# A new token order for q and for the stores, late last tokens, and a new condition in the planner of a linear-attention and SoLU kernel

## The chip, the cores and the metric

The kernel runs on one core of a Trainium2 chip. The metric is device time in microseconds (us). Before the change it was 197.02 us (median of three runs, 196.54 to 197.72). Engines are called as the profile calls them: PE is TensorE, PEld its weight loads, DVE VectorE, ACT ScalarE, POOL GpSimd (it issues the loads), SP SyncE (it issues crossbar transposes and most stores).

## The reference, cut to what matters

```python
# q, k, v: [8 batches, 8 heads, 576 tokens, 64]; w_in [512, 1024]; w_out [1024, 512]
kv  = einsum('bhsd,bhse->bhde', k, v)            # no softmax: one 64x64 matrix per head
o   = einsum('bhsd,bhde->bhse', q, kv)
o   = o / sqrt(mean(o*o, -1) + 1e-6) * g_norm
x   = o.transpose(0, 2, 1, 3).reshape(4608, 512) # rows are tokens
h   = x @ w_in
u   = h * softmax(h)
out = layernorm(u) * g_ln @ w_out                # fp32, 4608 x 512
```

## The kernel before

The 4,608 tokens are worked off in nine chunks of 512. Chunk c below 8 holds 512 tokens of batch c; chunk 8 collects the 64 tokens that each batch has left ("last tokens"). Each chunk gives four output tiles of 128 tokens x 512 fp32, 256 KB each. From chunk 4 on, q is turned by a crossbar transpose that SyncE issues. SyncE issues the stores too, all in one queue, in order.

A small planner decides the order: every piece of work has an engine, a length, a rank and the pieces that it needs, and `Plan.order` deals them out by modelled time, then rank.

```python
def load_q(b, hs):                      # runs of 4 tokens, 1 KB each
    nc.gpsimd.dma_start(
        T["q", b].rearrange("p h j d -> p h (j d)")[:, hs],
        q[b, :, 0:512, :].rearrange("h (p j) d -> p h (j d)", j=4)[:, hs])
...
behind = [] if b < 2 else [("h_mm", 0, 0)] if b == 2 else [("h_mm", b - 3, 2 if b == 3 else 0)]
...
def o_mm(c, hf, tag):                   # q times kv; four 64x64 quarters of PE in turn
    ...
    for b in [c] if c < B else range(B):
        cols = slice(0, 128) if c < B else slice(b, 128, B)     # chunk 8: 32 columns, strided
        ...
            nc.tensor.matmul(ts[z][..., pp, :, cols], kvd[rows, b, ...], T["qT", c][rows, ..., cols], ...)
...
def store(c, m):
    j = 2 * (m % 2) + m // 2
    if c < B:
        dst = out[c * S:c * S + 512, :].rearrange("(p j) d -> j p d", j=4)     # dst[j]: 128 x 512
    else:
        dst = out.rearrange("(b s) d -> b s d", b=B)[:, 512:S, :].rearrange("b (p j) d -> j p b d", j=4)
    (nc.scalar if c == NC - 1 and m % 2 else nc.sync).dma_start(dst[j], T["ob", c, m][:, :])
```

The softmax here doesn't subtract the row's maximum and nothing guards it: scores larger than these inputs give would overflow.

Of the kernel before, what the change touches and what calls it, by code (L numbers as in the profile page):

```python
# [89 lines left out]
def kernel(  # L90
# [57 lines left out]
    q_last = big.tile([128, H, 4, D], BF16, name="q_last")  # L148
# [64 lines left out]
    def load_kv(name, src, b, hs):  # L213

        if hs.start == 0:
            T[name, b] = tile_of((name, b), [128, NP, 9, D], BF16)
        nc.gpsimd.dma_start(  # L217
            T[name, b].rearrange("p n i d -> p n (i d)")[:, hs.start // 2:hs.stop // 2],
            src[b, hs].rearrange("(n r) (p i) d -> (r p) n (i d)", r=2, i=9),
        )  # L220

    def load_q(b, hs):
        if hs.start == 0:
            T["q", b] = tile_of(("q", b), [128, H, 4, D], BF16)
        nc.gpsimd.dma_start(  # L225
            T["q", b].rearrange("p h j d -> p h (j d)")[:, hs],
            q[b, :, 0:512, :].rearrange("h (p j) d -> p h (j d)", j=4)[:, hs],
        )

    def load_q_last(b):  # L230
        nc.gpsimd.dma_start(
            q_last[b:128:B].rearrange("p h j d -> p h (j d)"),
            q[b, :, 512:S, :].rearrange("h (p j) d -> p h (j d)", j=4),
        )
# [17 lines left out]
    for b in range(B):  # L252
        at = b - 9.0 if b > 1 else (-2.0, -1.5)[b]
        behind = [] if b < 2 else [("h_mm", 0, 0)] if b == 2 else [("h_mm", b - 3, 2 if b == 3 else 0)]
        for g, hs in enumerate(heads(b)):
            part = 0.1 * g
            n = len(heads(b))
            for i, (name, src) in enumerate((("k", k), ("v", v))):
                plan.add((name, b, g), "pool", 0.75 if n == 1 else 0.6, at + part + 0.01 * i,
                         lambda name=name, src=src, b=b, hs=hs: load_kv(name, src, b, hs),  # L260
                         behind, uses=[(name, b)] if g else [],
                         first=[] if g else [(name, b)], load=2.9 / n if b < 3 else 3.5)
            plan.add(("q", b, g), "pool", 0.9 if n == 1 else 0.7, at + part + (0.02 if b < 2 else 0.1),
                     lambda b=b, hs=hs: load_q(b, hs), behind,
                     uses=[("q", b)] if g else [], first=[] if g else [("q", b)], load=2.7 / n if b < 3 else 3.3)
        plan.add(("q_last", b), "pool", 0.6, 2.0 + 0.5 * b, lambda b=b: load_q_last(b),
                 [("h_mm", 2 + b // 2, 4 * (b % 2))], load=0.5)
# [45 lines left out]
    def qT_mm(c, hf, tag):  # L313

        t = T["qTp", c, hf] = bank((tag,), [128, 4, 2, 128], BF16)
        for h in range(4):
            for y in range(2):
                src = T["q", c][:, 4 * hf + h, 2 * y:2 * y + 2, :].rearrange("p z d -> p (z d)")
                nc.tensor.transpose(t[:, h, y, :], src, ident[:, :])

    def qT_copy(c, hf):
        if hf == 0:
            T["qT", c] = tile_of(("qT", c), [128, H, 2, 128], BF16)
        dst, src = T["qT", c][:, 4 * hf:4 * hf + 4], T["qTp", c, hf][:, :, :, :]
# [5 lines left out]
    def q_turn(c):  # L330

        t = T["qT", c] = tile_of(("qT", c), [128, H, 2, 128], BF16)
        nc.sync.dma_start_transpose(
            t.rearrange("q h y p -> q (h y) p"), T["q", c].rearrange("p h j d -> p (h j d)")
        )

    def o_mm(c, hf, tag):

        ts = [bank((tag,), [128, 2, 2, 128], FP32) for z in range(2)]
        for z in range(2):  # L340
            T["o", c, hf, z] = ts[z]
        for pp in range(2):
            for b in [c] if c < B else range(B):
                cols = slice(0, 128) if c < B else slice(b, 128, B)
# [345 lines left out]
```

## Time and profile before

| | before |
|---|---|
| time (median); span of the profiled run, which itself took 194.98 us | 197.02; 193.1 us |
| PE busy, granted clock | 179.8 us (93%), 0.998 |
| PE idle between its first and last matmul (gaps over 0.15 us) | 7.2 us |
| last matmul to the end | 4.25 us |

### The profile page before, as it was taken

The numbers are of one execution on the slowest core, as the hardware profiler recorded it, in microseconds if no ns is written. First come the engines' busy times: TensorE is split into PE (matmuls) and PEld (weight loads), VectorE is DVE, ScalarE is ACT, GpSimd is POOL, SyncE is SP. The second block draws the span as 40 slices with busy tenths as digits, with TensorE's granted clock in tenths as the row PEclk, the third lists the DMA queues.
The fourth block names the chain that finished last, engine by engine and source line by source line (L and its number), as shares of the span: only waits on it lengthen the run. The fifth ranks groups of instructions, "written<-read, shape, count | busy, mean of one in ns | idle before, by whom it ended". The sixth has DMA issues, their size and how long they took to land.

```text
span 193.1 us, 5442 instructions
## 1 busy us (share of the span) xinstructions
PE 179.8 (93%) x2282; PEld 88.3 (46%) x2282; DVE 122.6 (63%) x241; ACT 141.0 (73%) x245; POOL 127.9 (66%) x136
## 2 busy tenths in 40 slices
PE   7897997898899998999899999999999999999991
PEld 2352454553354643544354435445445554544460
DVE  1456588468684887496477658567575747666450
ACT  2038888869895997799689987989789496655520
POOL 7981799500999987977499776568285838846200
PEclk9999999999999999999999999999999999999999
DMA  1999999999996999899999996363111111211206
GB/s 22 204 204 266 357 203 205 206 224 248 233 201 86 147 190 258 113 185 168 292 214 200 212 111 182 108 116 114 54 54 58 58 54 58 109 58 54 110 7 213
DMA packets 36040, 29.71 MB, mean 154 GB/s; under 512 B 11816, under 2 KB 30512, under 8 KB 36016
## 3 DMA queue, kind: packets, MB, share of 16 engines
q0 software_dynamic: 20112, 17.30, 56.4%
q1 hardware_dynamic: 15616, 11.67, 22.4%
q10 hardware_dynamic: 288, 0.39, 0.6%
q8 instruction: 18, 0.29, 0.6%
q14 instruction: 6, 0.05, 0.1%
HBM read 32.51 MB, written 9.44 MB: 217 GB/s over the span
## 4 chain that ended last, share of the span: by engine, by line
PE 64%; DMA 20%; ACT 7%; POOL 4%; DVE 2%; issue 2%; SPq 0%; POOLq 0%; DVEq 0%; ACTq 0%
PE out_ps L582 26%; PE h_ps L468 24%; DMA w_out_f<-in_moe_w_out_dram 9%; DMA v_sb<-in_v_dram 7%; PE misc_ps L534 4%; DMA out_dram<-ob_sb 4%; PE s_ps L369 3%; PE o_ps L348 2%; ACT e_sb L476 2%; PE misc_ps L291 1%; DVE u_sb L483 1%; ACT osq_sb L363 1%; ACT rst_sb L377 1%; ACT lss_sb L373 1%; PE h_ps L592 1%
## 5 line engine op out<-in xcount | busy, mean ns | idle before, releaser
L468 PE MATMUL h_ps<-x_sb,w_in_sb 128*128 128x512 bf16 x276 | 70.3, 379 | 3.0 <-DVE u_sb L483 1.7
L582 PE MATMUL out_ps<-w_out_sb,u_sb 128*128 128x512 bf16 x272 | 69.0, 379 | 0.5 <-issue 0.5
L494 POOL TENSOR_TENSOR usq_sb<-u_sb 128x512 bf16<-128x512 bf16 x50 | 52.0, 1042 | 25.5 <-DVE u_sb L483 25.4
L483 DVE TENSOR_TENSOR u_sb<-h_ps,e_sb 128x512 bf16<-128x512 f32 x69 | 47.3, 688 | 30.4 <-ACT e_sb L476 29.5
L500 POOL TENSOR_TENSOR es_sb<-e_sb 128x512 bf16<-128x512 f32 x36 | 45.9, 1274 | 21.6 <-ACT e_sb L476 21.2
L476 ACT ACTIVATE e_sb<-h_ps,zero_t 128x512 f32<-128x512 f32 x69 | 47.1, 684 | 12.6 <-PE h_ps L468 11.8
L468 PEld LDWEIGHTS <-w_in_sb 128*128 128x128 bf16 x288 | 27.3, 98 | 37.5 <-issue 6.9
L582 PEld LDWEIGHTS <-u_sb 128*128 128x128 bf16 x280 | 26.1, 98 | 31.0 <-issue 2.0
L363 ACT ACTIVATE osq_sb<-o_ps,zero_t 128x512 bf16<-128x512 f32 x31 | 20.1, 683 | 15.3 <-PE o_ps L348 15.3
L614 DVE TENSOR_SCALAR ob_sb<-out_ps,rstd 128x512 f32<-128x512 f32 x33 | 24.6, 745 | 10.0 <-PE out_ps L582 4.3
L390 DVE SCALAR_TENSOR_TENSOR x_sb<-o_ps,g_rep,rst_sb 128x512 bf16<-128x512 f32 x32 | 23.9, 749 | 8.6 <-ACT rst_sb L377 8.4
L377 ACT ACTIVATE rst_sb<-lss_sb,zero_t 128x512 f32<-128x512 f32 x32 | 23.2, 726 | 0.7
L373 ACT ACTIVATE lss_sb<-s_ps,eps_t 128x512 f32<-128x512 f32 x32 | 22.0, 688 | 2.2 <-PE s_ps L369 2.2
L492 ACT ACTIVATE usq_sb<-u_sb,zero_t 128x512 bf16<-128x512 bf16 x22 | 15.8, 719 | 5.4 <-DVE u_sb L483 5.4
L369 PE MATMUL s_ps<-osq_sb,head_mean 128*128 128x512 bf16 x34 | 12.9, 380 | 0.3 <-ACT osq_sb L363 0.3
L534 PEld LDWEIGHTS <-stat_sel 128*32 128x32 bf16 x720 | 10.1, 97 | 3.8 <-issue 3.8
L217 POOL DMA_DIRECT2D k_sb<-in_k_dram x10 | 7.8, 784 | 4.3 <-DMA w_in_sb<-in_moe_w_in_dram 2.9
L198 PE MATMUL s_ps<-zeros 128*128 128x512 bf16 x28 | 9.2, 453 | 1.4 <-DVE zero_t L163 1.2
L225 POOL DMA_DIRECT2D q_sb<-in_q_dram x10 | 8.6, 856 | 2.5 <-DMA w_in_sb<-in_moe_w_in_dram 1.5
L348 PE MATMUL o_ps<-qT_sb,kvd 64*64 64x32 bf16 (+1 forms) x240 | 8.2, 256 | 1.1 <-DMA qT_sb<-q_sb 0.7
L291 PEld LDWEIGHTS <-k_sb 64*64 64x64 bf16 x576 | 6.7, 107 | 4.9 <-issue 4.9
L291 PE MATMUL misc_ps<-v_sb,k_sb 64*64 64x64 bf16 x360 | 7.6, 194 | 0.8 <-DMA v_sb<-in_v_dram 0.7
(85 smaller groups left out, 131.6 us busy)
## 6 DMA issues: line engine op xcount, KB each, us to landing
out_dram<-ob_sb SPq DMA_DIRECT2D x34, 256.0 KB, 2.9
k_sb<-in_k_dram POOLq DMA_DIRECT2D x6, 576.0 KB, 13.3
v_sb<-in_v_dram POOLq DMA_DIRECT2D x6, 576.0 KB, 14.3
q_sb<-in_q_dram POOLq DMA_DIRECT2D x6, 512.0 KB, 15.9
w_out_f<-in_moe_w_out_dram POOLq DMA_DIRECT2D x1, 2048.0 KB, 16.5
k_sb<-in_k_dram POOLq DMA_DIRECT2D x4, 288.0 KB, 11.5
v_sb<-in_v_dram POOLq DMA_DIRECT2D x4, 288.0 KB, 12.2
q_sb<-in_q_dram POOLq DMA_DIRECT2D x4, 256.0 KB, 12.2
```

Source lines behind the costliest of these rows:

```text
L363: nc.scalar.activation(out=t[:, :], in_=T[("o", *i)].rearrange("p a b c -> p (a b c)"), func=AF.Square, bias=zero_t[:, :])
L369: nc.tensor.matmul(t[:, :], head_mean[:, :], T["osq", i][:, :], start=True, stop=True)
L373: nc.scalar.activation(out=t[:, :], in_=T["s", i][:, :], func=AF.Ln, bias=eps_t[:, :])
L377: nc.scalar.activation(out=t.rearrange("p a b c -> p (a b c)"), in_=T["lss", i][:, :], func=AF.Exp, scale=-0.5, bias=zero_t[:, :])
L390: nc.vector.scalar_tensor_tensor(out=T["x", c][:, 2 * hf:2 * hf + 2, z], in0=T["o", c, hf, z][:, :, :, :], scalar=g_rep[:, :], in1=T["rst" ...
L468: nc.tensor.matmul(t[:, :], w_in_sb[:, dt, f * 128:(f + 1) * 128], T["x", c][:, dt].rearrange("p a b c -> p (a b c)"), start=(dt == 0), st ...
L476: nc.scalar.activation(out=T["e", c, f // 2][:, f % 2, :], in_=T["h", c, f][:, :], func=AF.Exp, bias=zero_t[:, :])
L483: nc.vector.tensor_tensor(out=T["u", c][:, f, :], in0=T["h", c, f][:, :], in1=T["e", c, f // 2][:, f % 2, :], op=MUL)
L494: nc.gpsimd.tensor_tensor(out=dst, in0=src, in1=src, op=MUL)
L500: nc.gpsimd.tensor_tensor(out=T["es", c][:, n, :], in0=e[:, 0, :], in1=e[:, 1, :], op=ADD)
L582: nc.tensor.matmul(T["acc", c, m][:, :], T["u", c][:, f, m * 128:(m + 1) * 128], w_out_sb[:, f, :], start=(f == 0), stop=(f == NF - 1),)
L614: nc.vector.tensor_scalar_mul(out=t[:, :], in0=T["acc", c, m][:, :], scalar1=T["rstd", c][:, m:m + 1])
```

## The change

The intent: longer runs of q (2 KB in place of 1 KB), the products of the last tokens without stride, the last tokens loaded later, and the loads of chunks 5 to 7 held back until the transpose ahead of them has been issued, because a transpose beside loads was seen to take 12 to 15 us (11.8 and 14.5 us from issue to landing, in the trace of before). Tokens are therefore dealt out in runs of nine (eight for the chunk, the ninth for chunk 8), and the stores follow that order. The core of the diff, cut:

```diff
-        nc.gpsimd.dma_start(
-            T["q", b].rearrange("p h j d -> p h (j d)")[:, hs],
-            q[b, :, 0:512, :].rearrange("h (p j) d -> p h (j d)", j=4)[:, hs],
+            src[b, hs].rearrange("(n r) (p j) d -> (r p) n (j d)", r=2, j=9)[:, :, 0:js * D],
     def load_q_last(b):
-            q_last[b:128:B].rearrange("p h j d -> p h (j d)"),
-            q[b, :, 512:S, :].rearrange("h (p j) d -> p h (j d)", j=4),
+        nc.gpsimd.dma_start(q_last[:, :, b, :], q[b].rearrange("(n r) (p j) d -> (r p) n j d", r=2, j=9)[:, :, 8, :])
...
-        behind = [] if b < 2 else [("h_mm", 0, 0)] if b == 2 else [("h_mm", b - 3, 2 if b == 3 else 0)]
+        behind = ... + ([("turned", b - 1)] if b - 1 in XBAR else [])
...
-        plan.add(("q_last", b), "pool", 0.6, 2.0 + 0.5 * b, ..., [("h_mm", 2 + b // 2, 4 * (b % 2))], load=0.5)
+        plan.add(("q_last", b), "pool", 0.7, 4.0 + 0.25 * b, ..., [("h_mm", 4 + b // 4, 2 * (b % 4))], load=0.7)
...
+            plan.add(("turned", c), "wait", 2.0, r - 0.05, lambda: None, [("q", c, 0)] if c < B else [])
...                                                   # o_mm: chunk 8 by run, 64 contiguous columns
-                cols = slice(0, 128) if c < B else slice(b, 128, B)
+            for y in [slice(0, 4)] if c < B else range(4):
...
+    def rows_of(c, z, y):
+        if c < B:
+            return out[c * S:c * S + S, :].rearrange("(p j) d -> j p d", j=9)[2 * y + z:2 * y + z + 3:2]
+        return out.rearrange("(b p j) d -> j b p d", p=64, j=9)[8, 2 * y + z:2 * y + z + 3:2]
     def store(c, m):
-        ... dma_start(dst[j], T["ob", c, m][:, :])          # 128 x 512
+        ... dma_start(rows_of(c, m // 2, 2 * (m % 2)), T["ob", c, m][:, :])   # 2 x 64 x 512
```

The two halves of the last tile of chunk 8 (`store_cols`) go through `rows_of` as well.

More of the change, by code (lines that the diff above doesn't have):

```diff
@@ L147 @@
     kvd = big.tile([128, B, 2, NP, D], BF16, name="kvd")
-    q_last = big.tile([128, H, 4, D], BF16, name="q_last")
+    q_last = big.tile([128, NP, B, D], BF16, name="q_last")
     g_rep = big.tile([128, 1], FP32, name="g_rep")
@@ L210, with load @@
     plan.add("ident", "pool", 1.0, -1.95, make_ident)
-    def load_kv(name, src, b, hs):
+    def load(name, src, b, hs):
+        js = 8 if name == "q" else 9
         if hs.start == 0:
-            T[name, b] = tile_of((name, b), [128, NP, 9, D], BF16)
+            T[name, b] = tile_of((name, b), [128, NP, js, D], BF16)
         nc.gpsimd.dma_start(
-            T[name, b].rearrange("p n i d -> p n (i d)")[:, hs.start // 2:hs.stop // 2],
-            src[b, hs].rearrange("(n r) (p i) d -> (r p) n (i d)", r=2, i=9),
-        )
-    def load_q(b, hs):
-        if hs.start == 0:
-            T["q", b] = tile_of(("q", b), [128, H, 4, D], BF16)
-        nc.gpsimd.dma_start(
-            T["q", b].rearrange("p h j d -> p h (j d)")[:, hs],
-            q[b, :, 0:512, :].rearrange("h (p j) d -> p h (j d)", j=4)[:, hs],
+            T[name, b].rearrange("p n j d -> p n (j d)")[:, hs.start // 2:hs.stop // 2],
+            src[b, hs].rearrange("(n r) (p j) d -> (r p) n (j d)", r=2, j=9)[:, :, 0:js * D],
         )
     def load_q_last(b):
-        nc.gpsimd.dma_start(
-            q_last[b:128:B].rearrange("p h j d -> p h (j d)"),
-            q[b, :, 512:S, :].rearrange("h (p j) d -> p h (j d)", j=4),
-        )
+        nc.gpsimd.dma_start(q_last[:, :, b, :], q[b].rearrange("(n r) (p j) d -> (r p) n j d", r=2, j=9)[:, :, 8, :])
     def load_w_in(half):
@@ L253 @@
         at = b - 9.0 if b > 1 else (-2.0, -1.5)[b]
-        behind = [] if b < 2 else [("h_mm", 0, 0)] if b == 2 else [("h_mm", b - 3, 2 if b == 3 else 0)]
+        behind = [] if b < 2 else [("h_mm", 0, 0)] if b == 2 else [("h_mm", b - 3, 2 if b == 3 else 0)] + ([("turned", b - 1)] if b - 1 in XBAR else [])
         for g, hs in enumerate(heads(b)):
@@ L257 @@
             n = len(heads(b))
-            for i, (name, src) in enumerate((("k", k), ("v", v))):
-                plan.add((name, b, g), "pool", 0.75 if n == 1 else 0.6, at + part + 0.01 * i,
-                         lambda name=name, src=src, b=b, hs=hs: load_kv(name, src, b, hs),
+            for i, (name, src) in enumerate((("k", k), ("v", v), ("q", q))):
+                plan.add((name, b, g), "pool", (0.8 if name == "q" else 0.75) if n == 1 else 0.6, at + part + (0.01 * i if i < 2 else 0.02 if b < 2 else 0.1),
+                         lambda name=name, src=src, b=b, hs=hs: load(name, src, b, hs),
                          behind, uses=[(name, b)] if g else [],
-                         first=[] if g else [(name, b)], load=2.9 / n if b < 3 else 3.5)
-            plan.add(("q", b, g), "pool", 0.9 if n == 1 else 0.7, at + part + (0.02 if b < 2 else 0.1),
-                     lambda b=b, hs=hs: load_q(b, hs), behind,
-                     uses=[("q", b)] if g else [], first=[] if g else [("q", b)], load=2.7 / n if b < 3 else 3.3)
-        plan.add(("q_last", b), "pool", 0.6, 2.0 + 0.5 * b, lambda b=b: load_q_last(b),
-                 [("h_mm", 2 + b // 2, 4 * (b % 2))], load=0.5)
+                         first=[] if g else [(name, b)], load=(2.55 if name == "q" else 2.9) / n if b < 3 else 3.2 if name == "q" else 3.5)
+        plan.add(("q_last", b), "pool", 0.7, 4.0 + 0.25 * b, lambda b=b: load_q_last(b),
+                 [("h_mm", 4 + b // 4, 2 * (b % 4))], load=0.7)
     for half in range(2):
@@ L313, in qT_mm @@
     def qT_mm(c, hf, tag):
-        t = T["qTp", c, hf] = bank((tag,), [128, 4, 2, 128], BF16)
-        for h in range(4):
-            for y in range(2):
-                src = T["q", c][:, 4 * hf + h, 2 * y:2 * y + 2, :].rearrange("p z d -> p (z d)")
-                nc.tensor.transpose(t[:, h, y, :], src, ident[:, :])
+        t = T["qTp", c, hf] = bank((tag,), [128, 2, 4, 128], BF16)
+        for n in range(2):
+            for y in range(4):
+                src = T["q", c][:, 2 * hf + n, 2 * y:2 * y + 2, :].rearrange("p z d -> p (z d)")
+                nc.tensor.transpose(t[:, n, y, :], src, ident[:, :])
     def qT_copy(c, hf):
         if hf == 0:
-            T["qT", c] = tile_of(("qT", c), [128, H, 2, 128], BF16)
-        dst, src = T["qT", c][:, 4 * hf:4 * hf + 4], T["qTp", c, hf][:, :, :, :]
+            T["qT", c] = tile_of(("qT", c), [128, NP, 4, 128], BF16)
+        dst, src = T["qT", c][:, 2 * hf:2 * hf + 2], T["qTp", c, hf][:, :, :, :]
         if c == 1:
@@ L330, in q_turn @@
     def q_turn(c):
-        t = T["qT", c] = tile_of(("qT", c), [128, H, 2, 128], BF16)
+        t = T["qT", c] = tile_of(("qT", c), [128, NP, 4, 128], BF16)
         nc.sync.dma_start_transpose(
-            t.rearrange("q h y p -> q (h y) p"), T["q", c].rearrange("p h j d -> p (h j d)")
+            t.rearrange("q n y p -> q (n y) p"), T["q", c].rearrange("p n j d -> p (n j d)")
         )
     def o_mm(c, hf, tag):
-        ts = [bank((tag,), [128, 2, 2, 128], FP32) for z in range(2)]
+        ts = [bank((tag,), [128, 2, 4, 64], FP32) for z in range(2)]
         for z in range(2):
@@ L342, in o_mm @@
         for pp in range(2):
-            for b in [c] if c < B else range(B):
-                cols = slice(0, 128) if c < B else slice(b, 128, B)
+            n = 2 * hf + pp
+            for y in [slice(0, 4)] if c < B else range(4):
                 for hh in range(2):
@@ L348, in o_mm @@
                         nc.tensor.matmul(
-                            ts[z][hh * 64:hh * 64 + 64, pp, :, cols], kvd[rows, b, hh ^ z, 2 * hf + pp, :],
-                            T["qT", c][rows, 4 * hf + 2 * pp + hh, :, cols], start=True, stop=True,
+                            ts[z][hh * 64:hh * 64 + 64, pp, y, :], kvd[rows, c if c < B else 2 * y + z, hh ^ z, n, :],
+                            T["qT", c][rows, n, y, 64 * hh:64 * hh + 64], start=True, stop=True,
                         )
@@ L375, in s_exp @@
     def s_exp(*i):
-        t = T["rst", i] = tile_of(("rst", i), [128, 2, 2, 128], FP32)
+        t = T["rst", i] = tile_of(("rst", i), [128, 2, 4, 64], FP32)
         nc.scalar.activation(
@@ L381, in s_rsqrt @@
     def s_rsqrt(*i):
-        t = T["rst", i] = tile_of(("rst", i), [128, 2, 2, 128], FP32)
+        t = T["rst", i] = tile_of(("rst", i), [128, 2, 4, 64], FP32)
         nc.scalar.activation(
@@ L388, in x_mul @@
         if (hf, z) == (0, 0):
-            T["x", c] = tile_of(("x", c), [128, NP, 2, 2, 128], BF16)
+            T["x", c] = tile_of(("x", c), [128, NP, 2, 4, 64], BF16)
         nc.vector.scalar_tensor_tensor(
@@ L429 @@
             kvs = [("kv", b, x, part) for b in ([c] if c < B else range(B)) for x in ((hf,) if b < 2 else range(2)) for part in range(3)]
-            plan.add(("o_mm", c, hf), "pe", 0.25 if c < B else 1.2, r + w * (0.35 + 0.5 * hf),
+            plan.add(("o_mm", c, hf), "pe", 0.25 if c < B else 0.6, r + w * (0.35 + 0.5 * hf),
                      lambda c=c, hf=hf, tag=tag: o_mm(c, hf, tag), [("qT", c) if c in XBAR else ("qT", c, hf), *kvs],
@@ L605, in store_cols @@
     def store_cols(x):
-        dst = out.rearrange("(b s) (x d) -> b s x d", b=B, x=2)[:, 512:S, x, :].rearrange("b (p j) d -> j p b d", j=4)[3]
-        (nc.sync, nc.scalar)[x].dma_start(dst, T["ob", NC - 1, 3][:, x])
+        cols = slice(x * d_model // 2, (x + 1) * d_model // 2)
+        (nc.sync, nc.scalar)[x].dma_start(
+            rows_of(NC - 1, 1, 2)[:, :, cols], T["ob", NC - 1, 3][:, x]
+        )
     def scale(c, m):
@@ L614, in scale @@
             nc.vector.tensor_scalar_mul(out=t[:, :], in0=T["acc", c, m][:, :], scalar1=T["rstd", c][:, m:m + 1])
+    def rows_of(c, z, y):
+        if c < B:
+            return out[c * S:c * S + S, :].rearrange("(p j) d -> j p d", j=9)[2 * y + z:2 * y + z + 3:2]
+        return out.rearrange("(b p j) d -> j b p d", p=64, j=9)[8, 2 * y + z:2 * y + z + 3:2]
     def store(c, m):
-        j = 2 * (m % 2) + m // 2
-        if c < B:
-            dst = out[c * S:c * S + 512, :].rearrange("(p j) d -> j p d", j=4)
-        else:
-            dst = out.rearrange("(b s) d -> b s d", b=B)[:, 512:S, :].rearrange("b (p j) d -> j p b d", j=4)
-        (nc.scalar if c == NC - 1 and m % 2 else nc.sync).dma_start(dst[j], T["ob", c, m][:, :])
+        (nc.scalar if c == NC - 1 and m % 2 else nc.sync).dma_start(
+            rows_of(c, m // 2, 2 * (m % 2)), T["ob", c, m][:, :]
+        )
     plan.add("w_mean", "pe", 2.0, -0.5, lambda: [w_mean(f) for f in range(NF)], ["w_out", "g_mean", ("o_mm", 0, 1)],
```

## The prediction

> **What bounds the kernel now.** I read the page first: shares by engine, then the chain that ended last, then PE's gaps in the timeline, then each DMA's issue and landing, because the change touches loads, crossbar transposes and stores.
>
> ```profile
> PE 179.8 (93%) x2282; PEld 88.3 (46%) x2282; DVE 122.6 (63%) x241; ACT 141.0 (73%) x245; POOL 127.9 (66%) x136
> ```
>
> PE is the bound: 179.8 of a 193.1 us span, at a granted clock of 0.998. The other 13.3 us are 1.2 before the first matmul, 4.25 after the last one (188.87 to 193.12: last scaling and last stores), and gaps inside. From the timeline the gaps over 0.15 us add to 7.2 us, and 5.3 of those lie before 48 us. What ended the gaps that the change could touch, from the view of waits:
>
> ```profile
> PE misc_ps L291 <- DMA v_sb<-in_v_dram: 0.7, 1, 0.7
> PE o_ps L348 <- DMA qT_sb<-q_sb: 0.7, 1, 0.7
> DVE ob_sb L614 <- DMA out_dram<-ob_sb: 2.0, 1, 2.0
> ```
>
> The second is chunk 5's crossbar transpose (gap at 94.3 us). The third is its after-effect: VectorE waits for a store, and PE loses 0.37 us more at 96.6. SyncE's timeline from 60 to 100 us shows why:
>
> ```profile
> 61.37 1.70 SPq L333 DMA_TRANSPOSE qT_sb<-q_sb  x1
> 68.02 5.04 SPq L623 DMA_DIRECT2D out_dram<-ob_sb  x3
> 80.37 7.29 SPq L333 DMA_TRANSPOSE qT_sb<-q_sb  x1
> 87.76 3.44 SPq L623 DMA_DIRECT2D out_dram<-ob_sb  x4
> ```
>
> The transpose at 61.37 meets chunk 5's loads (issued 61.58 to 63.99) and lands after 11.8 us, chunk 5's q only at 80.32; the next transpose meets chunk 6's loads (78.43 to 80.88) and lands after 14.5 us. The one of the last chunk, with the queue empty, lands after 4.3. So the intent is sound, and worth about 0.67 + 0.37 = 1.04 us.
>
> Now the stores, which the diff changes only in passing. Windows of the trace: one around a single store, one with only stores running, one in the stage of loads.
>
> ```profile
> 138.10:139.00 0.90, 0.90 (x6) 0.42 (x5) 0.14 (x1) 0.90 (x2) 0.00 (x0) 1.00 0.75 291
> 140.00:165.00 25.00, 25.00 (x308) 12.47 (x307) 16.67 (x29) 19.16 (x33) 16.64 (x15) 1.00 0.14 55
> 5.00:35.00 30.00, 26.27 (x355) 13.64 (x353) 18.74 (x32) 19.11 (x32) 23.41 (x28) 1.00 1.28 239
> ```
>
> The last two columns are the mean busy share of the 16 DMA engines and GB/s. One 256 KB store takes 0.75 x 0.9 us = 0.675 us of all sixteen, so 10.8 engine-us. That agrees with the packet records: 128 packets of 2 KB at a median 84 ns, eight to an engine, one behind the other. (1 KB packets: 46 ns.) In the stage of loads the engines are full.
>
> [...] the small load of the norm weights has 8 rows outermost, and its semaphore gets one update at 2.66 us and eight at 6.08 to 6.32, with eight data packets and eight completion packets. Ordinary stores have 128 outermost, those of the last chunk 16 (16 x 8 rows): 16 updates each. [...] the first store (38.67 us), beside loads, needs 6.7 us for eight packets per engine, some 0.7 us a packet[...]; alone a store lands in 2.0 us. [...] 64 matmuls of 32 columns take 1.06 us of PE's chain, 8 of 256 columns (as many columns in all) 0.34.
>
> **The change, part by part.**
>
> *The last chunk's products.* 2 x 64 matmuls of 32 columns, read at a stride, become 2 x 32 of 64 contiguous columns. At the same time per instruction (1.06/64 = 16.6 ns) a group takes 0.53 us; the floor is 0.34. PE saves 2 x 0.53 to 0.72, say 1.2 us, all on the path.
>
> *q in runs of eight.* 512 rows of 2 KB per chunk replace 1,024 of 1 KB. In the loads alone (chunk 4) v takes 2.79 us between landings, q 2.66; at v's rate per byte (1.18 MB against 1.05 MB) q would take 2.5. So 0.15 us per chunk: PE's 0.72 us wait for chunk 2's v shrinks by two such, 0.3 us, of which a dependency behind it may eat part. I count 0.2.
>
> *Last tokens.* 8 DMAs of 128 rows of 1 KB become 8 of 512 rows of 256 B, issued later. From 60 ns (1,024 B) and 107 ns (2,304 B) per packet a straight line gives about 32 ns: 32 packets per engine, 1.0 us each, an estimate. Before, the transpose of these tokens landed at 131 and was used at 144.5, so 10 us of room remain.
>
> *Loads behind the transpose.* In the built order chunk 5's and 6's loads move behind one more square and one more sum on GpSimd (1.03 + 1.26 = 2.3 us); a transpose alone needs 4.3, so most of the collision goes: the 1.04 us above.
>
> So far 197.0 - 1.2 - 0.2 - 1.0 = 194.6 us.
>
> *The stores.* The 128 rows of a tile are now tokens 2y+z and 2y+z+2 of 64 runs, and the built stores have an output pattern of 2 x 64 x 512 where before it was 128 x 512 (or 16 x 8 x 512). [...] k = 2, and always the same two engines. One store is then 64 packets per engine, 64 x 84 ns = 5.4 us, where PE delivers a tile every 4.3 us (17.3 us per chunk of four). All work of these two engines from the first store (38.7 us, first packet 0.9 later):
> - stores: 35 x 64 x 84 ns = 188.2, two half ones 2 x 64 x 46 ns = 5.9: 194.1 us
> - loads still to come: 2.5 (chunk 2's q) + 5 x 8.0 = 42.5 (every load needs all engines, these two as well)
> - last tokens: 8.0; five transposes, 128 packets of 256 B per engine at 18 ns: 5 x 2.3 = 11.5
> Sum 256.1. Loads and stores add rather than overlap: between 41.4 and 53.3 us loads worth 8.2 us took 11.9 with four stores beside them, 0.9 us a store where 0.67 is its own time.
>
> Do these engines rest? Four output buffers and two PSUM banks let PE run six tiles ahead at most, so the ring always holds stores; a transpose stands in the ring behind up to four of them (21.5 us), and PE waits for it in order. Only SyncE's hand-over after each of five transposes lets them idle: 3 us in all, my guess. 38.7 + 0.9 + 256.1 + 3 = 298.7 us of span; time is 3.9 above the span before (197.0 against 193.1), so 302.6, rounded to 303. PE's gains vanish behind that.
>
> **The rivals.** (a) [...] For: the change is plainly meant for a gain; no store in this trace has an outermost 2. Against: the 8-row load is split by eight [...]. Time 194.6. (b) Two engines, but other ones for each store. A store lands after 0.8 + 5.4 + 0.4 = 6.6 us instead of 2.0; four buffers at 4.3 us each tolerate 17, so only the tail grows by some 5: about 200. [...] (c) Two engines, and more starvation than I count: packets at 90 or 100 ns, idle at each transpose. 10 ns more is 35 x 64 x 0.01 = 22 us: 325. (d) Faster packets in long runs: at 76 ns, -18 us: 285.
>
> **Range and chances.** I give k = 2 on fixed engines 0.8. Within it (c) and (d) span 285 to 325; I widen to 275 to 330. The rest goes mostly to (a), which lies within 2% (193.1 to 201.0) more often than under it, and (b).
>
> **What would show it.** Right: stores of 256 KB that land after 6 us or more everywhere (before: 2.0 to 2.4 in the quiet part), with two completion packets each; DMA share about 2/16 = 0.12 throughout the second half, while GB/s stays near 49; PE below 65% busy, its waits on DVE's scaling and on qT_sb; DVE's scaling waiting on out_dram. Matmul groups of the last chunk at about 0.5 us show the first step, chunk 5's q landing well before 80 us (in case (a)) the fourth. Wrong: stores still landing after 2 us; then the time is 194 to 196, and the step that failed is the choice of engines. If two engines are used and the time is under 260, the failed step is that their work adds up without overlap.

Passages on the hardware that no trace of this case shows have been cut from the prediction. Its sum came to 38.7 + 0.9 + 256.1 + 3 = 298.7 us of span, 302.6 as a time. What goes is the reason for k = 2 (k is the number of DMA engines that carry one store). That an outermost 2 means two engines, the same two for every store, was the assumption. Rival (a) is that this form of the stores does no harm.

## More of the kernel before

The prediction shows the lines on PE's share and its waits. Here are the other lines that the change will move, from the page of the kernel before: the busy tenths of PE and of the DMA engines and PE's granted clock, each in 40 slices of the span, then the queue that SyncE's stores and transposes use (packets, MB, share of 16 engines' time), then the chain that ended last.

```profile
PE   7897997898899998999899999999999999999991
PEclk9999999999999999999999999999999999999999
DMA  1999999999996999899999996363111111211206
...
q1 hardware_dynamic: 15616, 11.67, 22.4%
...
PE 64%; DMA 20%; ACT 7%; POOL 4%; DVE 2%; issue 2%; SPq 0%; POOLq 0%; DVEq 0%; ACTq 0%
```

PE is full from end to end, and the DMA engines are full in the first 60% of the span and nearly idle after (1 is 10 to 20%).

## The result, and the profile after

The changed kernel is correct and takes 294.06 us (median of four runs, 293.47 to 295.06); the kernel before took 197.37 us in the same rounds. The ratio is 1.4925 (95% interval 1.4843 to 1.5007). A run counts as slow when it is over 1.5% above the fastest run of its kernel, and as fast otherwise. Ratios here are always the mean time of one kernel's fast runs over the mean of the other's fast runs of the same rounds, so they are not quite the ratio of the medians.

The page of the kernel after, in the same order as the lines of before:

```profile
PE 194.3 (67%) x2218; PEld 92.0 (32%) x2218; DVE 122.4 (42%) x241; ACT 142.2 (49%) x245; POOL 128.7 (44%) x136
...
PE   7889797999224991099708966994599798630000
...
PEclk9999999999955897559986997899599999785555
DMA  6999999919915399579474296178311111111111
...
q1 hardware_dynamic: 15126, 11.67, 34.0%
...
DMA 75%; PE 8%; DVE 4%; ACT 2%; POOL 2%; issue 1%; SPq 0%; DVEq 0%; POOLq 0%
```

The span grew by 98.6 us (193.1 to 291.7), in three parts. PE's gaps add to 61.8 us (before 7.2): +54.6. The last matmul ends at 257.98, so the tail is 33.7 us (before 4.25): +29.5. And PE is busy 14.5 us longer for fewer products, because the granted clock sinks after gaps (the row of clocks; the mean over the span, tail included, is 0.846, and a 128x512 matmul of the first layer takes 408 ns on average in place of 379). The chain has turned from PE (64%) to DMA (75%).

The trace's sixteen clock records are 1.0 or 0.5, none between, and the last window below has 0.50 with no matmul at all. A value between, in a slice or a window, is a mean of the two.

The waits that ended those gaps (who waited for what: us in total, times, longest):

```profile
DVE ob_sb L605 <- DMA out_dram<-ob_sb: 67.4, 18, 8.0
...
PE o_ps L335 <- DMA qT_sb<-q_sb: 33.9, 4, 13.7
PE h_ps L457 <- DVE u_sb L472: 12.3, 6, 5.6
...
PE o_ps L335 <- DMA qT_sb<-q_last: 6.5, 1, 6.5
```

DVE waits 67.4 us for an output buffer, that is for a store to finish, where before it was once 2.0 us; PE waits 33.9 us for the crossbar transposes of the chunks (before 0.7) and 6.5 us for that of the last tokens. SyncE's timeline (start, length, source line, what, count) shows that both are one thing:

```profile
70.20 18.22 SPq L320 DMA_TRANSPOSE qT_sb<-q_sb  x1
88.53 9.61 SPq L615 DMA_DIRECT2D out_dram<-ob_sb  x4
98.25 23.07 SPq L320 DMA_TRANSPOSE qT_sb<-q_sb  x1
121.41 4.87 SPq L615 DMA_DIRECT2D out_dram<-ob_sb  x3
126.39 23.49 SPq L320 DMA_TRANSPOSE qT_sb<-q_sb  x1
```

A transpose stands 13 to 23 us at SyncE (all five; 1.6 to 7.3 before), behind the stores that were issued ahead of it: with the stores cut in two and all else as here (experiment 2) it is 1.6 to 7.1 us. And the windows of 20 us (busy time by engine, then clock, DMA share, GB/s), first a stretch with only stores and PE running, then one in the tail:

```profile
220.00:240.00 20.00, 18.48 (x160) 8.66 (x159) 11.64 (x22) 11.87 (x20) 12.31 (x11) 1.00 0.14 52
...
260.00:280.00 20.00, 0.00 (x0) 0.00 (x0) 0.82 (x2) 1.16 (x2) 0.00 (x0) 0.50 0.13 51
```

In the tail nothing runs but stores, and the sixteen DMA engines are 0.13 busy: two of sixteen, moving 51 GB/s. A tile of 256 KB at 51 GB/s takes 5.1 us.

How many engines carry a store can be read from the packets. Data packets of the stores are as many as before (4,352 of 2 KB). The queue lost 15,616 - 15,126 = 490 packets = 35 stores x 14, all of them packets of 4 bytes (888 before, 398 after): each of SyncE's 35 stores sends two completion packets and not sixteen. (ScalarE's queue lost 28, two stores x 14.) The same count is used in the experiments.

### The profile page after: what moved, and what is told of

It reads as the page before. It is cut to its first block, busy times and chain, and to the rows that moved or that the text cites. A ratio compares the mean times of both kernels' runs of the same rounds, so it can differ in the third digit from the quotient of the medians.

```text
span 291.7 us, 5310 instructions
## 1 busy us (share of the span) xinstructions
PE 194.3 (67%) x2218; PEld 92.0 (32%) x2218; DVE 122.4 (42%) x241; ACT 142.2 (49%) x245; POOL 128.7 (44%) x136
## 3 DMA queue, kind: packets, MB, share of 16 engines
q1 hardware_dynamic: 15126, 11.67, 34.0%
## 4 chain that ended last, share of the span: by engine, by line
DMA 75%; PE 8%; DVE 4%; ACT 2%; POOL 2%; issue 1%; SPq 0%; DVEq 0%; POOLq 0%
DMA out_dram<-ob_sb 60%; DMA qT_sb<-q_sb 7%; DMA qT_sb<-q_last 5%; DMA v_sb<-in_v_dram 2%; PE out_ps L571 2%; PE h_ps L457 2%; DVE ob_sb L605 1%; DVE u_sb L472 1%; POOL k_sb L218 1%; DVE w_out_sb L562 1%; PE misc_ps L198 1%; PE out_ps L556 1%; PE o_ps L457 1%; DVE x_sb L377 1%; PE o_ps L335 1%
## 5 line engine op out<-in xcount | busy, mean ns | idle before, releaser
L457 PE MATMUL h_ps<-x_sb,w_in_sb 128*128 128x512 bf16 x276 | 77.2, 408 | 13.7 <-DVE u_sb L472 12.3
L571 PE MATMUL out_ps<-w_out_sb,u_sb 128*128 128x512 bf16 x272 | 75.1, 401 | 4.1 <-DVE u_sb L472 3.2
L457 PEld LDWEIGHTS <-w_in_sb 128*128 128x128 bf16 x288 | 28.6, 103 | 53.0 <-issue 26.7
L571 PEld LDWEIGHTS <-u_sb 128*128 128x128 bf16 x280 | 27.1, 101 | 38.6 <-issue 7.8
L335 PE MATMUL o_ps<-qT_sb,kvd 64*64 64x256 bf16 (+1 forms) x176 | 7.8, 275 | 41.1 <-DMA qT_sb<-q_sb 33.9
L335 PEld LDWEIGHTS <-kvd 64*64 64x64 bf16 x192 | 4.0, 116 | 49.0 <-issue 41.4
L356 PE MATMUL s_ps<-osq_sb,head_mean 128*128 128x512 bf16 x34 | 13.9, 409 | 0.6 <-ACT osq_sb L350 0.6
L523 PEld LDWEIGHTS <-stat_sel 128*32 128x32 bf16 x720 | 11.1, 103 | 4.4 <-issue 4.4
L218 POOL DMA_DIRECT2D q_sb<-in_q_dram x10 | 7.5, 749 | 3.2 <-DMA w_in_sb<-in_moe_w_in_dram 1.4
## 6 DMA issues: line engine op xcount, KB each, us to landing
w_out_f<-in_moe_w_out_dram POOLq DMA_DIRECT2D x1, 2048.0 KB, 16.5
```

The lines of the kernel that those rows point to most:

```text
L218: nc.gpsimd.dma_start(T[name, b].rearrange("p n j d -> p n (j d)")[:, hs.start // 2:hs.stop // 2], src[b, hs].rearrange("(n r) (p j) d -> ...
L457: nc.tensor.matmul(t[:, :], w_in_sb[:, dt, f * 128:(f + 1) * 128], T["x", c][:, dt].rearrange("p a b c -> p (a b c)"), start=(dt == 0), st ...
L571: nc.tensor.matmul(T["acc", c, m][:, :], T["u", c][:, f, m * 128:(m + 1) * 128], w_out_sb[:, f, :], start=(f == 0), stop=(f == NF - 1),)
```

## The experiments

The first two questions: is it really the outermost size of the store, and what do the other parts do when the stores are mended? Then: does one slow store hurt, or only many; what is the tail worth; is the planner's condition good; and what would be a good version?

### 1. The outermost size alone, on the kernel before

```diff
+        rows = dst[j]
+        if c < B:
+            rows = rows.rearrange("(p a) d -> a p d", a=2)      # also a=4, a=8
-        ... dma_start(dst[j], T["ob", c, m][:, :])
+        ... dma_start(rows, T["ob", c, m][:, :])
```

The 128 rows of a tile are only walked in another order, so the result is wrong; everything else is the kernel before. Chunk 8 keeps its own pattern.

> The kernel before, its layout and order untouched, with the stores of chunks 0 to 7 given an outermost 2 (output pattern 2 x 64 x 512: every second row in each half; the rows land permuted, so the result is wrong on purpose). Theory: two engines carry 32 stores of 5.0 us (the rate seen after), 160 us, beside 43 us of loads, 4 of last tokens and 11.5 of transposes, from 43 us on: some 262 us of span, time 258 to 278. If the form of the stores is not the cause but the layout of q or the order: 196 to 199.

> The same with an outermost 4 (4 x 32 x 512, rows permuted, wrong on purpose). Theory: four engines, 2.5 us a store; PE makes a tile in 4.3 us, so these engines have 80 + 58 = 138 us of work in the 150 us after the first store and are no longer the bound, but some transposes and loads come later: 197 to 206 us. If an outermost dimension under 16 is a penalty of its own (not a share of engines): as slow as with 2, over 255.

> Before, its stores' 128 rows walked as 8x16x512 (rows permuted, so a wrong result on purpose); third point of the dose. If eight engines take a store (16 packets each, 16 x 80 ns = 1.3 us + 1.4 us of latency) it lands after about 2.7 us in the quiet part in place of 2.0-2.3, transposes behind it land later by under a microsecond each: 196-199, ratio 1.005-1.02, where two engines gave 1.415 and four 1.098. Rival: the outermost size acts only through a threshold (a store slower than the interval between tiles), and eight is as good as 128: 0.995-1.005.

| outermost size (chunks 0 to 7) | time, us | ratio to before (95%) | packets lost by SyncE's queue |
|---|---|---|---|
| 128 (before) | 195.62 / 195.74 | 1 | 0 |
| 8 | 202.99 (200.49 to 211.91) | 1.0333 (1.0268 to 1.0398) | 256 = 32 x 8 |
| 4 | 214.12 (213.07 to 216.00) | 1.0983 (1.0913 to 1.1054) | 384 = 32 x 12 |
| 2 | 275.89 (274.88 to 276.50) | 1.4149 (1.4080 to 1.4218) | 448 = 32 x 14 |

(Sizes 4 and 2 ran beside runs of before at 195.62 us, size 8 beside 195.74.) The queue's line in the pages of 8, 4 and 2:

```profile
q1 hardware_dynamic: 15360, 11.67, 30.8%
```

```profile
q1 hardware_dynamic: 15232, 11.67, 32.6%
```

```profile
q1 hardware_dynamic: 15168, 11.67, 32.8%
```

The bytes are the same in all, and each store of 32 sends exactly 8, 4 or 2 completion packets: the outermost size is the number of engines. Size 2 alone, on the old kernel, gives 80 us of the 97. That settles the main cause.

My expectations for 4 and 8 were too low. I had thought of the mean load of the engines; what counts is the stage in which loads run too. Worked out afterwards, as an estimate, for one of the engines used and one chunk of 17.3 us: loads 8.0, one transpose 2.3, last tokens 1.1 (2.3 such loads a chunk, 8 packets an engine at 60 ns each), and four stores at 128/k packets of 80 ns each: 2.6, 5.1, 10.2 or 20.5 us for 16, 8, 4 and 2 engines. The sums are 14.0, 16.5, 21.6 and 31.9 us, so 81%, 95%, 125% and 184% of the chunk. At 125% the four chunks of this stage must lose 4 x 4.3 = 17 us; 18.5 were measured. At 95%, by this estimate, only queueing is left, and the kernel lost 7 us. In both, part of the loss is PE's clock, which falls after a wait (0.957 to 0.964 in the runs of size 4, 0.982 to 0.990 in the fast ones of size 8), so the 17 is closer to the 18.5 than the estimate deserves. The view of waits for size 4 shows where the loss is felt:

```profile
PE o_ps L348 <- DMA qT_sb<-q_sb: 13.9, 3, 4.7
...
DVE ob_sb L614 <- DMA out_dram<-ob_sb: 7.1, 1, 7.1
```

PE waits three times for a transpose, 4.7 us each at most, although over all the chunks together the engines have time enough (138 us of work in 150, in my expectation). (The profile of size 8 fell in its slowest execution, so I read only its counts.)

### 2. The change with each store cut in two

```diff
-        engine.dma_start(dst, T["ob", c, m][:, :])
+        for i in range(2):                                      # 64 x 512 each; store_cols likewise
+            engine.dma_start(dst[i], T["ob", c, m][64 * i:64 * i + 64, :])
```

> The changed kernel with each store cut in two of 64 rows (outermost 64 instead of 2), nothing else. Theory (the 2 x 64 x 512 form puts every store on the same two DMA engines, and these are the bound): stores land after 2 to 3 us again, with 16 completion packets each, PE over 92% busy, time 194.6 us by the steps of the prediction, 193.5 to 197. Rival A (the loads of q in runs of eight, or the last tokens in 256 B rows, choke the DMA engines): still 280 to 295. Rival B (the new order makes the crossbar transposes wait): still over 250, with PE waiting for qT_sb.

197.86 us (six runs, 192.71 to 199.02), correct, above the 193.5 to 197 that I expected; stores land after 2.2 to 2.4 us in the quiet part. Five of the six runs are over 1.5% above the fastest and count as slow, the profiled one (197.58) too, so there is no ratio. But the 97 us are gone, with the change otherwise whole. What is left is not the gain that I had counted on, and the next run says why.

### 3. The same without the planner's condition

```diff
-        behind = ... + ([("turned", b - 1)] if b - 1 in XBAR else [])
+        behind = ...                                            # as before
```

> The cut stores without the planner's new condition (loads of chunks 5 to 7 no longer behind the transpose of the chunk ahead). If the order is worth what the prediction says (0.67 + 0.37 us of PE's waits at one transpose), this is about 1.0 us slower than the cut stores alone, and a transpose beside loads lands after more than 10 us again. If the order is worth nothing: within 0.3 us.

194.03 us (193.39 to 194.43, six fast runs), ratio 0.9939 (0.9904 to 0.9974). So the condition does not save the microsecond. Whether it costs something can't be told from this pair alone: the medians are 3.8 us apart, but five of the six runs with the condition count as slow, and the sixth (192.71) is below all six here. The fast runs of experiment 4 show that it costs; the traces show how. Lines of SyncE's timeline, first with the condition (experiment 2), then without:

```profile
79.75 1.60 SPq L320 DMA_TRANSPOSE qT_sb<-q_sb  x1
...
96.84 7.06 SPq L320 DMA_TRANSPOSE qT_sb<-q_sb  x1
```

```profile
75.67 3.19 SPq L320 DMA_TRANSPOSE qT_sb<-q_sb  x1
...
92.73 2.58 SPq L320 DMA_TRANSPOSE qT_sb<-q_sb  x1
```

With the condition, the transpose of chunk 4 is indeed short (it lands after 3.7 us in place of 15.0). But the loads of chunk 5, held back until 65.0 us, land at 79.7 in place of 75.3, those of chunk 6 at 96.8 in place of 92.7, and then chunk 6's transpose is issued at 96.84, in the middle of chunk 7's loads (96.65 to 98.2), and lands after 15.9 us in place of 4.6. PE waits for it, in the view of waits of experiment 2:

```profile
PE o_ps L335 <- DMA qT_sb<-q_sb: 2.6, 1, 2.6
```

PE loses more than this wait. A window of the same trace (columns as before: busy time by engine, clock, DMA share, GB/s) shows the clock after it:

```profile
114.00:118.00 4.00, 4.00 (x12) 1.50 (x11) 1.44 (x2) 2.32 (x4) 0.74 (x2) 0.59 1.84 233
```

The clock is at half for 3.4 us, from 113.8 us on, which costs some 1.7 us more (half of that stretch, an estimate). In the profile without the condition PE never waits for a transpose, and the clock is full until after the last matmul. One collision was moved from a place with slack to a place without.

### 4. The condition alone, on the kernel before

```diff
+        behind = ... + ([("turned", b - 1)] if b - 1 in XBAR else [])
+            plan.add(("turned", c), "wait", 2.0, r - 0.05, lambda: None, [("q", c, 0)] if c < B else [])
```

> The kernel before with only the planner's new condition (the loads of chunks 5 to 7 put behind the crossbar transpose of the chunk ahead); layout and stores of before. My prediction's step: 1.0 us faster than before, 194.6, ratio 0.995. Theory after e1_split against e3_no_turn (197.9 against 194.0): the condition makes a load wait where it need not, the transpose itself then lands no earlier, and it costs 1 to 4 us, at least in part of the executions: 196.5-199.5, ratio 1.005-1.02, with a gap of TensorE of over 1.5 us before an o_mm that waits for qT.

198.12 us (196.38 to 199.89, six runs, two of them slow), ratio 1.0148 (1.0089 to 1.0207) to a kernel before at 194.80. These are fast runs against fast runs, so here the condition's cost is shown, and the profiled execution (198.01) is a fast one. It is the same picture on the old layout: chunk 6's transpose issued at 99.44 among chunk 7's loads (96.5 to 99.0), landing after 13.3 us, and one new gap of PE of 2.75 us at 110.06, with the clock at half for 3.4 us after it. The two fast runs with a mean clock of 0.988 and 0.991 took 198.0 and 198.2 us, the two with 0.996 and 0.997 took 196.4 and 196.9, so the fall of the clock seems to come in some executions and not in others.

```profile
99.44 6.59 SPq L333 DMA_TRANSPOSE qT_sb<-q_sb  x1
```

### 5. The place of the last tokens alone

```diff
-        plan.add(("q_last", b), "pool", 0.7, 4.0 + 0.25 * b, ..., [("h_mm", 4 + b // 4, 2 * (b % 4))], load=0.7)
+        plan.add(("q_last", b), "pool", 0.7, 2.0 + 0.5 * b, ..., [("h_mm", 2 + b // 2, 4 * (b % 2))], load=0.7)
```

This is experiment 3 with the last tokens loaded as early as before.

> e3_no_turn (194.0 us) with the last tokens loaded as early as before (one from chunk 2 on, at before's places in the plan); tests the part 'last tokens loaded late' alone. Theory: those eight loads carry 0.26 MB of 9.4 MB of loads after 38 us and the transpose that waits for them has 10 us of room either way, so the place is worth nothing that is not lost again: 193.5-195, within 0.5% of e3. Rival (the intent): loaded early they stand in front of chunk 5 to 7's loads and each delays a transpose by about 1 us: 195-197, with a gap of TensorE over 0.5 us before an o_mm that waits for qT.

195.29 us (194.87 to 196.45), ratio 0.9987 (0.9950 to 1.0025), against 0.9939 with late loading. The intervals overlap a little, and the two ran on different chips, so the half per cent is likely rather than proved. The profile speaks for the rival: chunk 4's transpose lands at 77.5 in place of 76.0, and PE has the gap that the rival named.

```profile
PE o_ps L335 <- DMA qT_sb<-q_sb: 1.6, 1, 1.6
```

So this part of the change likely does what it is meant to.

### 6. Uncut stores in one chunk only, and in the last chunk only

```diff
-        if True:                    # experiment 3: all stores cut in two
+        if c != 6:                  # e5_mid: chunk 6's four stores uncut
+        if c < NC - 1:              # e6_tail: only chunk 8's stores uncut, halves included
```

> The kernel e3_no_turn (all stores cut in two) with the four stores of chunk 6 alone left uncut, as the change writes them. Theory: the time of the change comes from stores that pile up, 5.0-5.1 us each on two engines against one store about every 4.6 us that the rest of the kernel would make, so what counts is the total and not one slow store; four of them (20 us of two engines) at about 144 to 165 us find no transposes or loads behind them and nobody waits: 194-195.5 us against e3's 194.0, ratio to before 0.992-1.000, and those four stores' landing 6 to 9 us after their issue in place of 2.3. Rival: a single slow store already holds the kernel up (its ob buffer, or the chain of stores), each costing its 2.8 us more: 194+11=205 us.

> The kernel e3_no_turn with only the last chunk's stores left uncut (three whole tiles and two halves, from two queues). Theory: [...] the last chunk's 1 MB leaves at 5.1 us a store from its first issue (184.4 in e3): 184.4 + 1.5 + 4 x 5.1 = 206.3 in place of 190.5, so about 210 us, 208-212, ratio 1.06-1.09 to before. Rival: the two queues use different engines (two each), then 2 stores of 5.1 a queue: end at about 197, time about 200.

With chunk 6 uncut: 193.61 us (192.47 to 193.66), ratio 0.9940 (0.9888 to 0.9992). Nothing is lost. Its four stores in SyncE's timeline, 11.14 us from the first issue to the last, with no transposes and no loads behind them:

```profile
153.59 11.14 SPq L621 DMA_DIRECT2D out_dram<-ob_sb  x4
```

By their completion packets these four landed 7.7, 8.7, 9.4 and 12.4 us after their issue (6 to 9 expected), and in the view of waits nobody waits for them.

With chunk 8 uncut: 211.28 us (211.04 to 220.98), ratio 1.0859 (1.0797 to 1.0920). The fast runs are 211.2 - 194.0 = 17.2 us above those of experiment 3 (which ran on another chip), where four stores of 5.1 us in a row, both queues on the same two engines, had led me to expect 16. The stores come from two queues here, SyncE's and ScalarE's; a window in the tail (of the profiled execution, which was the slow one of the four) shows that this gives no more engines:

```profile
196.00:216.00 20.00, 0.00 (x0) 0.00 (x0) 0.00 (x0) 0.47 (x1) 0.00 (x0) 0.60 0.13 48
```

Again 0.13, two of sixteen. So four slow stores in the quiet part are harmless. Slow stores cost where transposes or loads need their engines (experiment 1), or where they come last.

### 7. One store a tile on all engines: two attempts that gave nothing

The destination can be walked as 64 x 2 x 512, rows outermost, if a tile's partition is (row, run) and not (run, row). For that the columns of o_mm must come in another order, either where PE writes them (e7) or where it reads them (e9; its chunk 8 is as in e7):

```diff
-            return out[...].rearrange("(p j) d -> j p d", j=9)[2 * y + z:2 * y + z + 3:2]
+            return out[...].rearrange("(p j) d -> p j d", j=9)[:, 2 * y + z:2 * y + z + 3:2]
 # e7: write PSUM at a stride of two fp32;  e9: read qT in the order h p l, write contiguously
+            to.rearrange("m (h p l) -> m h l p", h=2, l=2)[:, hs, ls], ..., turned[rows, hs, ls, hh]
+            to.rearrange("m (h p l) -> m h p l", h=2, l=2), ..., turned[rows, :, :, hh].rearrange("q h l p -> q h p l")
```

> The change without the planner's condition, one store a tile again, its destination walked as 64x2x512 (rows outermost, the two token residues inside), so that the outermost size is 64 and not 2; o_mm writes PSUM in the order that this needs, a tile's partition is (row, residue). Theory: all 16 engines take each store, as with 128x512; the doubled issues of e3 fall away (its tail from the last matmul to the end was 5.55 us against 4.25 before): 192-194 us, ratio 0.982-0.994 to before. Rival: two strided rows inside an outer row make a slower store (3 us or more in place of 2.3), or o_mm's permuted writes slow the matmuls: 194-197.

> e7_interleave with the reordering moved from o_mm's PSUM write (columns at a stride of two fp32) to its moving operand (columns read in the order that is wanted, PSUM written contiguously); stores again 64x2x512, one a tile. In e7 the 112 matmuls of 64x256 took 408 ns each where e3_no_turn's took 281, 3.1-3.2 us more of TensorE, which ate what the single stores gave. Theory: the strided PSUM write is what is slow; read contiguous or not, a column costs the same: 281 ns again, last matmul at 186 in place of 188.6, time 191-192.5, ratio 0.978-0.990. Rival: the strided read of the moving operand costs the same or more: 400 ns or more a matmul, 194 or later.

Both are correct, with all sixteen engines (15,616 packets), and with a tail of 3.7 us. But e7 takes 194.14 us (ratio 0.9982, 0.9940 to 1.0024) and e9 194.99 (0.9969, 0.9941 to 0.9998), no better than cutting each store. The groups of products by form (count, then busy us and mean ns), of experiment 3, e7 and e9:

```profile
L335 PE MATMUL o_ps<-qT_sb,kvd 64*64 64x256 bf16 x112 | 6.1, 281 | 0.7 <-ACT qT_sb L313 0.5 <-DVE x_sb L377 0.3
```

```profile
L338 PE MATMUL o_ps<-qT_sb,kvd 64*64 64x256 bf16 x112 | 9.2, 408 | 0.6 <-ACT qT_sb L313 0.5 <-DVE x_sb L381 0.2
```

```profile
L342 PE MATMUL o_ps<-qT_sb,kvd 64*64 64x256 bf16 x112 | 9.9, 413 | 0.6 <-ACT qT_sb L313 0.5
```

281 ns became 408 and 413: PE reaches its last matmul at 188.64 and 189.36 us in place of 186.35, which eats the shorter tail. Both times my theory was wrong and the rival right: with e7's stride of 8 bytes in PSUM a product took 408 ns, with e9's of 256 bytes in SBUF 413.

### 8. The good parts together

Experiment 3 with the order of e7 in the last chunk only: chunks 0 to 7 are stored in two cuts, chunk 8 in one DMA a tile, 64 x 2 x 512.

```diff
+            if c < B: to = to[:, y, :]
+            else:     to = to.rearrange("m y p -> m (y p)").rearrange("m (h p l) -> m h l p", h=2, l=2)[:, y // 2, y % 2]
-        if True:
+        if c < NC - 1:              # cut in two
```

> The candidate for a version better than both: e3_no_turn with the last chunk's stores written once each, as 64x2x512 (all sixteen engines), its 64 products written to PSUM in the order that this needs, and the stores of chunks 0 to 7 cut in two as in e3. Theory: the extra issues of e3 cost only in the tail (5.55 us from the last matmul to the end, against 3.7 in e7 and e9), while the slow strided products of e7 and e9 (112 x 130 ns of TensorE) are avoided except for 64 small ones (243 ns in place of 195): tail 3.7-4.0, time 192.3-193.3, ratio to before 0.984-0.992. Rival: the tail is not set by the issues, or the start of the last chunk moves back as much: 194, ratio 0.994.

191.97 us (191.71 to 198.02, six runs, one of them slow), ratio 0.9855 (0.9802 to 0.9908): 1.4% faster than before, so within 2% of it, but outside the noise, and the lowest median of all variants (a little under the 192.3 to 193.3 that I expected). From its page:

```profile
span 190.2 us, 5327 instructions
...
PE 177.0 (93%) x2191; PEld 88.2 (46%) x2218; DVE 122.7 (65%) x241; ACT 141.1 (74%) x245; POOL 128.5 (68%) x136
```

The last matmul ends at 186.46 (before 188.87), and the tail is 3.7 us (before 4.25, experiment 3 5.51). (2,191 of 2,218 matmuls are in the records, so PE's busy time is a little low.)

## Why the prediction was right, and where it was off

**The stores: right, and mis-sized by a few per cent.** Two engines, always the same ones, for every store: shown by the packet counts, by the share of 0.13 with one queue and with two (0.14 in the change while several stores were under way: those issued from 217 to 251 us landed 16.8 to 19.6 us after their issue, one every 5.1 us), and by size 2 alone on the old kernel. The sum of the prediction was 39.6 + 256.1 + 3 = 298.7 us of span; the trace has the first store packet at 43.1 and the last ending at 290.2, with 1.5 us to the end. The term that was too large is the store: packets come every 80 ns while only stores run (84 ns is how long one takes, and they overlap a little), so a store is 5.1 us and not 5.4, and 35 of them with the two halves 185.1 and not 194.1. With the other terms as they were (62.0) that is 247.1; between first and last packet 247.1 went by. So the guess of 3 us of idleness was not needed. Together 303 became 294: 302.6, less 9.0 for the stores and 3 for the idleness, plus 3.5 for a first packet that came later than I had it and 1.5 for the end, less 1.5 for the step from span to time.

Two of the prediction's terms, the first packet and the step from span to time, rest on misreadings of the profile of before. (1) I put the first packet 0.9 us after the first store's issue, as in the quiet part. The trace of before has it at 42.19 us, 3.5 us after the issue at 38.67. So the 6.7 us to its landing are not eight packets at 0.7 us each: once begun, the store's packets came within 1.9 us. In the changed kernel the two engines begin a store packet every 0.17 to 0.18 us each while loads run beside it, against 0.08 alone. (2) The 3.9 us from span to time set the median of some runs against the span of another: the profiled execution of before took 194.98 us for its 193.1, that of after 293.57 for 291.7, so the step is 1.9 in both, and 2.4 from this span to the median.

That loads and stores add on these engines, rather than overlap, is the step that carried the prediction, and 247.1 against 247.1 bears it out only if the terms for loads and transposes, which I took from before, hold here too. They were not measured again, so agreement this close is partly luck.

**The DMA share of 0.12 throughout the second half: only at its end.** From 220 us on the windows of 20 us have 0.13 and 0.14; from 140 to 220 they have 0.22 to 0.84, because loads, transposes and last tokens still ran there.

**PE below 65% busy: missed narrowly** (67%). The share is of a longer busy time: 14.5 us more through the lower clock, which I had not counted.

**Products of the last chunk: right, a little better.** The two groups took 1.13 and 1.14 us before and take 0.45 and 0.44 in experiment 3: 1.4 us saved, against 1.2. In the change itself the first took 0.64, at a lower clock.

**q in runs of eight: too small to see.** In chunk 4, between v's landing and q's, 2.66 us became 2.62 (experiment 3) and 2.53 (e7), where I had 2.5 expected; PE's wait for chunk 2's v varies from 0 to 1.3 us between variants.

**Last tokens: the size was right, the role was not.** A packet takes 32.5 ns on average (estimate 32). But I gave their place in the order no worth, since the transpose that needs them has 10 us of room. (In the changed kernel that room was gone: PE waited 6.5 us for it.) Experiment 5 speaks for a worth that lies elsewhere: early ones stand in front of other chunks' transposes, likely for about 1 us.

**Loads behind the transpose: wrong.** I wrote "most of the collision goes: the 1.04 us above". The collision of chunk 4's transpose went, and the next loads came later for it, so that chunk 6's transpose met chunk 7's loads. The test that I had set for this step, chunk 5's q landing well before 80 us, failed in the experiments with the condition: 79.7 in both (80.3 before). The step that failed is that I looked at the wait that would go and not at what the later loads would run into. Rival (a), 194.6 us if the stores did no harm, therefore came out near 198 in experiment 2, and near 194 without the condition.

Of the rivals, (a), no loss from the form of the stores, falls with the packet counts; (b), other engines for each store, falls with the constant share of 0.13 and with the tail of e6; (c), packets of 90 to 100 ns, did not come; (d), faster packets, held in direction (80 ns).

What stays open: the kernel before too has executions of 198 to 203 us among those of 194 to 196, with a clock of 0.98 to 0.99. They may be the same collision of a transpose with loads, falling one way or the other by chance, with the fall of the clock behind it; no profile of such an execution of before was taken. The slow runs of experiment 2 are open in the same way: one of them was profiled.

## What to carry to other kernels

Read the outermost size of every DMA pattern before anything else about it: a view that splits 128 rows into 2 x 64 moved the same bytes on two engines here, and cutting it in two DMAs, or turning the order, gave the sixteen back (in experiment 3 and in e7). What a slow transfer costs must be read where it runs: four slow stores in a quiet stretch cost nothing, the same four at the end 17 us, and in the stage of loads they held up every transpose behind them (13 to 23 us at SyncE). And when a piece of work is moved out of one collision, follow it to the next one before counting the gain.

## What else these runs measured

- What the outermost size of a store cost, in a kernel whose DMA engines are 81% busy (my estimate above) in the stage of loads: 1.033 with eight engines, 1.098 with four, 1.415 with two.
- How long a crossbar transpose takes beside other DMAs, with sixteen-engine stores: one of 128 x 2,048 bf16 (chunks 4 to 7) landed 11.8 and 14.5 us after its issue in before, 15.0 in experiment 3, 15.9 in experiment 2 and 13.3 in experiment 4, where a chunk's first load was issued in the 3 us ahead of it or within 0.3 us after it. It landed after 7.7 and 5.5 us in before, 3.7 in experiment 2 and 4.6 in experiment 3, where that load came 2.9 us later or more, or not at all. Behind two-engine stores in its own queue it stood 13 to 23 us at SyncE.
- What a stride cost these products: those of 64x256 went from 281 (experiment 3) to 408 ns with a stride of 8 bytes in PSUM (e7), and to 413 with a stride of 256 bytes in the moving operand (e9); those of 64 columns, with the stride in PSUM, from 195 to 243.
- When the clock fell: in the trace of the changed kernel it changes only at steps of 3.41 us. Of the steps at full clock up to the last matmul, each of the 8 in which PE was idle for 61% or more (by the modelled ends of its matmuls) was followed by half clock, and none of the 50 others, with 48% or less, was; nor was any of the 54 in before, with 42% or less. So a gap of 2.1 us was enough where it fell within one step.
